# Two blocks of W2 converted inside the attention loop, on ScalarE and VectorE

## The chip, the cores and the metric

One of the cores of a Trainium2 chip runs the program; nothing is shared with other cores. The metric is the time of one execution on the device, in microseconds, taken as the median of several runs.

## The reference

Three layers follow one another on 4 batches of 576 tokens:

```python
# 1. attention, 8 heads of 64, causal window of 64
scores = q @ k.T / 8, masked to 0 <= i - j < 64
x = softmax(scores) @ v                               # [4, 576, 512]
# 2. gated unit with a spatial product
h = relu(x @ w_in); u, v = h[..., :512], h[..., 512:]
v = normalised(v) over its channels
x = (u * (w_spatial @ v + b)) @ w_out
# 3. mixer: tokens, then channels
u = x + w_tok2.T @ relu(w_tok1.T @ x)                 # per batch, over tokens
return u + relu(u @ w_c1) @ w_c2                      # w_c1 [512, 1536], w_c2 [1536, 512]
```

The weights arrive as 64-bit floats. The kernel multiplies in fp32 halves: every operand x is split into a high part hi (x rounded to fp32r) and a low part lo = x - hi, and a product takes three matmuls, hi·hi, hi·lo and lo·hi.

## The kernel before

**From 64-bit words to halves.** A weight tile comes by DMA as pairs of 32-bit words. `down` (L71, ScalarE) scales the high words as floats, `to_f32` (L60, VectorE) turns that into fp32 with one shift over the whole tile (L63) and two bit operations for each half of it (L68, L69), and `split` (L147) makes hi on ScalarE and lo on VectorE or GpSimd.

**Seven products for four.** The last product with w_c2, called W2 here, is done by quadrants of 256 columns with seven products in place of eight. So each of its six blocks j (rows 128j and 128(j+6) of W2, 128x1024 values) is not only converted: `load_c2` (L728) also forms four sums and differences of its quadrants (L738, GpSimd), splits all eight slots (hi on ScalarE, lo on GpSimd, L149), and stores hi and lo to a scratch tensor `scr` in DRAM (L742), from where `product` (L889) reads them (`w<-scr`). The raw words, the values and the halves live in 8 rotating buffers of 4 KB a partition, the pool `k4`. w_c1 has six such blocks too (`load_c1`, L699).

**Stages.** In the profiled execution:

- 0 to about 230 us: the attention with the first product of layer 2 woven in. This loop (L528) is written in the order in which each engine executes it (`manual_schedule`, L463). There are 18 tiles; turn n transposes the probabilities of tile n on TensorE (`att_turn`, L276), copies them (PT, L286, ScalarE), takes the eight exponentials of tile n+1 (`sexp`, L261, ScalarE), normalises tile n+1 (`snorm`, L267, VectorE: rs L272, L273, pb L274), multiplies tile n by v (`att_pv`, L289), and begins tile n+2 (`scores`, `smax`). So `snorm` waits on VectorE for the exponentials, and the next turn's transposes wait for `snorm`. Parts of w_spatial (ws, L101, L103) are converted at the ends of turns 2 to 5. Matmuls of `uv_v`, `uv_u` and `spatial` fill the rest of TensorE.
- about 230 to 364 us: the product with w_out (`wout`), the transposes back (`x2nat`), the token mixer (`tok1`, `tok2`), and beside them the conversion of w_t1, w_t2 and of nearly all blocks of w_c1 and W2. Here a scheduler sets the order on each engine; `load_c1` and `load_c2` are given a lower priority (`later`, L692). The list at L601 is the order in which the raw blocks are fetched.
- from about 364 us: the channel mixer, in three passes over 768 tokens.

The scheduler also puts work of the second stage into the engines' queues of the first where it fits: the first five pieces of w_out are fetched and converted (raw, val, wo_h, wo_l) during the attention.

`U` (L58) holds u of layer 2 for the four batches. Its columns 1152 to 2176 serve as landing space for raw w_in at the start (L460) and are written again by `uv_u` of the second pair of batches, from turn 12 on.

Of the kernel before, what the change touches and what calls it, by code (L numbers as in the profile page):

```python
# [20 lines left out]
P = 128  # L21
# [14 lines left out]
def tile_kernel(ctx, tc, qT, kT, kE, v, w_in, wsT, b_sp, w_out, w_t1, w_t2, w_c1, w_c2, outT):  # L36

    nc = tc.nc
# [32 lines left out]
    def down(x, high):  # L71
        nc.scalar.activation(out=x, in_=f(high), func=AF.Copy, scale=DOWN)
# [386 lines left out]
    def wv_part(k):  # L459
        return w_part(U[:, k, 1152:2176], w_in[128 * k:128 * k + 128, 512:].unsqueeze(1), wi_h[:, k:k + 1, 512:], wi_l[:, k:k + 1, 512:], 512)  # L460

    E = mybir.EngineType
    with tc.manual_schedule(engines={E.PE, E.SP, E.Activation, E.DVE, E.Pool}):  # L463
        wv = [wv_part(k) for k in range(4)]
# [2 lines left out]
        def go(*ws):  # L467
            for w in ws:
                next(w, 0)
# [54 lines left out]
        keep_busy(7, psa.tile([P, 512], F32, tag="xo", name="xo", bufs=1))  # L524
        uv_v(*its[0])
        conv, late = {1: (0,), 2: (1, 2), 3: (3,)}, ()
        ws_at = {2: 2, 3: 2, 4: 3, 5: 3}
        for n in range(1, len(its)):  # L528
            more, some = n + 2 < len(its), n + 1 < len(its)
            cv = [wu[i] for i in conv.get(n, ())]  # L530
            if n > 1:
                if n + 3 < len(its):
                    load_qk(n + 3)
                if more:
                    load_v(n + 2)
            PT = att_turn(n, busy={1: 2, 2: 8}.get(n, 0))
            go(*late)
            go(*late)
            go(*cv[:1])
            go(*cv[:1])  # L540
            if some:
                sexp(n + 1, 0)
                sexp(n + 1, 1)
                snorm(n + 1)
            go(*cv[:1])
            go(*cv[:1])
            tick()
            left = BUDGET - run_work(1)
            go(*cv[1:])
            att_pv(n, PT)  # L550
            go(*cv[1:])
            if more:
                scores(n + 2)
                smax(n + 2, 0)
                smax(n + 2, 1)
            if n > 1:
                tick()
            late = cv[1:]
            while work and left > 0:
                left -= run_work(1)  # L560
                tick()
            load_ws(ws_at.get(n, 0))
            enable(n)
        while turns:
            tick()
# [25 lines left out]
    def c1_source(j):  # L591
        return [w_c1[:, 128 * r:128 * r + 128].rearrange("(k p) c -> p k c", p=P) for r in (j, j + NJ)]

    def c2_source(j):
        return [w_c2[128 * r:128 * r + 128, :] for r in (j, j + NJ)]

    HW, TW, NJ = 384, 768, 6
    sources = [([w_t1[128 * k:128 * k + 256, :].rearrange("(k p) c -> p k c", p=P)], {}) for k in (0, 2)]
    sources += [([w_t1[512:, :]], dict(rows=64, dup=True))]
    sources += [([w_t2[128 * k:128 * k + 128, c0:c0 + 288]], {}) for k in range(2) for c0 in (0, 288)]  # L600
    sources += [(c1_source(j) if w == 1 else c2_source(j), {}) for w, j in  # L601
                ((2, 0), (1, 0), (2, 1), (2, 2), (1, 1), (1, 2), (2, 3), (1, 3), (2, 4), (1, 4), (1, 5), (2, 5))]
    issued = []

    def issue_next():
# [76 lines left out]
                mm3(ps[:, :288], [(ht[b][j][0][:, dc], ht[b][j][1][:, dc], t2_h[:, j, cs], t2_l[:, j, cs]) for j in range(2)])  # L682
                nc.vector.tensor_tensor(out=us, in0=ps[:, :288], in1=us, op=ALU.add)

    scr = tc.dram_tile([8, NJ // 2, P, 2, 2, 256], F32, name="scr")
    sums = tc.dram_tile([NJ, P, 4, 256], F32, name="sums")
    c1 = {}

# [39 lines left out]
    def load_c2(j):  # L728
# [5 lines left out]
        def blk(s, n=1):  # L734
            return Y[s // 4][:, s % 4:s % 4 + n, :]

        for o, a, b, op in ((4, 1, 3, ALU.add), (5, 4, 0, ALU.subtract), (6, 0, 1, ALU.subtract), (7, 2, 5, ALU.subtract)):
            nc.gpsimd.tensor_tensor(out=blk(o), in0=blk(a), in1=blk(b), op=op)  # L738
        for s, n in ((0, 1), (2, 2), (4, 2), (6, 2)):
            hl = kp.tile([P, 2, 2, 256], F32R, tag="k4", name="hl", bufs=8)[:, :n]  # L740
# [33 lines left out]

    wout(0)
    run_work(len(work))
    load_c2(0)
    wout(1)
    x2nat(0)
    load_c1(0)  # L780
    wout(2)
    tok1(0)
    load_c2(1)
    x2nat(1)
    wout(3)
    tok2(0)
    load_c2(2)
    load_c1(1)
    wout(4)
    x2nat(2)  # L790
# [261 lines left out]
```

## Time and profile before

| | |
|---|---|
| median of 3 runs | 638.13 us (638.07 to 638.38) |
| the profiled execution: time, span | 638.47 us, 636.7 us |
| TensorE (PE) busy | 610.3 us, 96% of the span |
| VectorE (DVE) busy | 459.5 us, 72% |
| ScalarE (ACT) busy | 334.1 us, 52% |
| GpSimd (POOL) busy | 153.4 us, 24% |
| granted TensorE clock | 1.00 (2.4 GHz) in all slices but the last |

Busy time counts an engine's own instructions. A row of the timeline gives the start, the duration, the engine, the line, the operation, the tiles as out<-in, and in brackets the idle time before it and what ended that. Matmuls overlap, so their durations are latencies, not costs. SyncE (SP) issues all DMAs in order; an issue row that lasts long is one that waited.

### The profile page before, as it was taken

What the parts mean: (1) busy time and instruction counts of PE and PEld (TensorE: products, weight loads), DVE (VectorE), ACT (ScalarE), POOL (GpSimd) and SP (SyncE); (2) the same over time, 40 slices, a digit from 0 to 9 for tenths busy, and PEclk for the clock granted to TensorE, in tenths of its full rate; (3) what the DMA queues carried; (4) which work ended last, traced back from release to release, by engine and by line L of the source; (5) the groups of instructions that cost most, each with busy time, mean ns of one, the idle gap of its engine ahead of it and who ended that gap; (6) DMA issues with size and microseconds to landing.
All of it is one profiled execution on the core that took longest, in us unless ns stands there. A gap on an engine that the chain in (4) does not pass through costs nothing.

```text
span 636.7 us, 12004 instructions
## 1 busy us (share of the span) xinstructions
PE 610.3 (96%) x4455; PEld 566.8 (89%) x4455; DVE 459.5 (72%) x977; ACT 334.1 (52%) x839; POOL 153.4 (24%) x166
## 2 busy tenths in 40 slices
PE   5889999999999999999899999999999999999997
PEld 2568798998889899888788899999999999999987
DVE  4896857556584688769978951278875998867982
ACT  4777853545674464666554442345543646344550
POOL 5610000100010010565475471041000440002510
PEclk9999999999999999999999999999999999999999
DMA  8853473222330135557756455057433675534772
GB/s 325 271 158 112 152 235 127 78 77 75 102 116 2 34 118 158 177 193 248 256 183 218 183 174 218 0 198 257 149 125 133 220 230 196 178 103 151 255 248 75
DMA packets 46106, 103.60 MB, mean 163 GB/s; under 512 B 4192, under 2 KB 16736, under 8 KB 46048
## 3 DMA queue, kind: packets, MB, share of 16 engines
q1 hardware_dynamic: 46048, 102.84, 48.3%
q8 instruction: 35, 0.57, 0.4%
q14 instruction: 23, 0.19, 0.1%
HBM read 83.95 MB, written 18.87 MB: 162 GB/s over the span
## 4 chain that ended last, share of the span: by engine, by line
PE 64%; DVE 14%; ACT 7%; DMA 5%; issue 4%; POOL 3%; SPq 1%; DVEq 0%; ACTq 0%; POOLq 0%
PE mm L161 27%; PE A L904 17%; PE mm L833 8%; PE A L833 6%; ACT pb L264 3%; DMA U<-in_w_in 3%; POOL k L738 2%; DVE k L68 2%; DVE k L69 2%; PE xo L297 2%; PE pt L285 2%; DMA scr<-hl 2%; DVE k L63 1%; PE A L161 1%; PE sc L241 1%
## 5 line engine op out<-in xcount | busy, mean ns | idle before, releaser
L904 PE MATMUL A<-oh,w 128*128 128x384 f32 x480 | 102.7, 334 | 0.0
L886 POOL TENSOR_TENSOR H<-H 128x384 f32<-128x384 f32 x36 | 45.0, 1264 | 184.9 <-DVE ol L899 171.0
L899 DVE TENSOR_TENSOR ol<-H,oh 128x384 fp32r<-128x384 f32 x120 | 77.2, 676 | 16.4 <-ACT oh L898 12.7
L904 PEld LDWEIGHTS A<-oh,w 128*128 128x128 f32 x480 | 85.0, 188 | 0.0
L898 ACT CAST oh<-H 128x384 fp32r<-128x384 f32 x120 | 60.0, 514 | 41.5 <-PE A L904 31.0
L904 PE MATMUL A<-ol,w 128*128 128x384 f32 x240 | 61.4, 336 | 2.2 <-DVE ol L899 2.2
L161 PE MATMUL mm<-ws,nh 128*128 128x288 f32 x320 | 62.0, 297 | 0.4 <-DVE tmp L394 0.4
L161 PEld LDWEIGHTS mm<-ws,nh 128*128 128x128 f32 x320 | 49.9, 188 | 1.0 <-DVE tmp L394 0.6
L363 POOL TENSOR_SCALAR rstd<-mv 128x1 f32<-128x1 f32 x18 | 4.9, 272 | 178.4 <-DVE mv L362 178.3
L904 PEld LDWEIGHTS A<-ol,w 128*128 128x128 f32 x240 | 43.1, 188 | 3.3 <-DVE ol L899 3.2
L886 DVE TENSOR_TENSOR H<-H 128x384 f32<-128x384 f32 x36 | 22.6, 628 | 21.8 <-ACT H L826 19.6
L161 PE MATMUL mm<-ws,nl 128*128 128x288 f32 x128 | 37.7, 295 | 0.0
L264 ACT ACTIVATE pb<-pb,nm 128x128 f32<-128x128 f32 x96 | 37.3, 400 | 0.4 <-DVE nm L255 0.4
L286 ACT COPY PT<-pt 128x512 f32<-128x512 f32 x36 | 19.4, 591 | 31.5 <-PE pt L285 31.5
L272 DVE TENSOR_SCALAR rs<-sm 128x8 f32<-128x8 f32 (+1 forms) x19 | 3.3, 172 | 42.9 <-ACT pb L264 42.9
L161 PE MATMUL mm<-xh,wi_h 128*128 128x384 f32 x96 | 32.7, 341 | 0.7 <-ACT vf L357 0.6
L161 PE MATMUL mm<-xh,wi_l 128*128 128x384 f32 x96 | 32.1, 334 | 0.0
L161 PE MATMUL mm<-xl,wi_h 128*128 128x384 f32 x96 | 32.1, 334 | 0.0
L161 PE MATMUL mm<-gh,wo_h 128*128 128x512 f32 (+1 forms) x80 | 29.4, 378 | 0.1
L161 PE MATMUL mm<-gh,wo_l 128*128 128x512 f32 (+1 forms) x80 | 29.4, 370 | 0.0
L161 PE MATMUL mm<-gl,wo_h 128*128 128x512 f32 (+1 forms) x80 | 29.4, 370 | 0.0
L149 POOL TENSOR_TENSOR hl<-k,hl 128x512 fp32r<-128x512 f32 (+1 forms) x24 | 28.6, 1208 | 0.0
(190 smaller groups left out, 1691.4 us busy)
## 6 DMA issues: line engine op xcount, KB each, us to landing
w<-scr SPq DMA_DIRECT2D x63, 512.0 KB, 4.4
k<-in_w_c SPq DMA_DIRECT2D x24, 512.0 KB, 5.3
scr<-hl SPq DMA_DIRECT2D x18, 512.0 KB, 6.1
kk<-in_kT SPq DMA_DIRECT2D x16, 384.0 KB, 4.7
k<-sums SPq DMA_DIRECT2D x12, 512.0 KB, 3.2
qq<-in_qT SPq DMA_DIRECT2D x18, 256.0 KB, 4.0
va<-in_v SPq DMA_DIRECT2D x18, 256.0 KB, 2.9
vb<-in_v SPq DMA_DIRECT2D x18, 256.0 KB, 3.9
```

The source lines that it names most:

```text
L68: nc.vector.scalar_tensor_tensor(out=y, in0=high, scalar=-0x80000000, in1=y, op0=ALU.bitwise_and, op1=ALU.bitwise_or)
L69: nc.vector.scalar_tensor_tensor(out=y, in0=low, scalar=29, in1=y, op0=ALU.logical_shift_right, op1=ALU.bitwise_or)
L149: eng.tensor_tensor(out=lo, in0=x, in1=f(hi), op=ALU.subtract)
L161: nc.tensor.matmul(o, a, c, start=(i == 0), stop=(i == n - 1))
L264: nc.scalar.activation(out=pb[:, h, :], in_=scs[g][:, h - 4 * g, :] if mk is None else pb[:, h, :], func=AF.Exp, scale=SCALE if mk is None ...
L285: nc.tensor.transpose(pt[:, h, :], pb[:, 4 * g + h, :], ident)
L286: nc.scalar.copy(out=PT[:, 4 * g:4 * g + 4, :], in_=pt)
L833: nc.tensor.matmul(o, a, m, start=first and i == 0, stop=i == len(todo) - 1, skip_group_check=True)
L886: eng.tensor_tensor(out=out, in0=a, in1=b, op=ALU.subtract)
L898: nc.scalar.copy(out=oh, in_=blk[j])
L899: nc.vector.tensor_tensor(out=ol, in0=blk[j], in1=f(oh), op=ALU.subtract)
L904: nc.tensor.matmul(acc[d], a, m, start=(first and j == 0 and i == 0), stop=(last and j == NJ - 1 and i == 2), skip_group_check=True)
```

## The change

Blocks 0 and 1 of W2 are no longer converted by `load_c2` in the second stage. A new generator `early_c2(j)` does each in seven steps, and the table `at` in the attention loop sets the turn and the point in the turn for each step: for block 0 the load at the end of turn 2, `down` in the middle of turn 3, `to_f32` ahead of the exponentials and `snorm` of turn 4, the four sums at that point of turn 5, the hi copies in the middle of turn 5, the lo differences at the exponentials of turn 6, and the stores to `scr` in the middle of turn 6; block 1 the same, four turns later. The sums and differences that were GpSimd's are VectorE's there. Raw words, values and halves all lie in the free columns of `U`, the halves in the space of the raw words and values that they replace; so block 1 can be loaded only when the first stores of block 0 have been read out. A block takes six stores in place of four, of rows of 1 KB in place of 2 KB. The other four blocks of W2 and the six of w_c1 keep their order, and the calls `load_c2(0)` and `load_c2(1)` are gone.

```diff
+    C2_SUMS = ((4, 1, 3, ALU.add), (5, 4, 0, ALU.subtract), (6, 0, 1, ALU.subtract), (7, 2, 5, ALU.subtract))
+    def early_c2(j):
...
+        for r, src in zip(raw, c2_source(j)):
+            nc.sync.dma_start(out=r, in_=src.bitcast(I32))
...
+        yield
+        for i, (low, high) in enumerate(parts):
+            down(span(2, 2 * i, 2), high)
+        yield
+        to_f32(span(2, 0, 4), parts)
+        yield
+        for o, a, b, op in C2_SUMS:
+            nc.vector.tensor_tensor(out=val[o], in0=val[a], in1=val[b], op=op)
+        yield
+        homes = ((2, 2, 0, 0, 2), (4, 2, 0, 2, 2), (6, 2, 1, 0, 2), (0, 1, 1, 2, 1))
+        for s, n, r, at, w in homes:
+            nc.scalar.copy(out=span(r, at, n).bitcast(F32R), in_=span(2 + s // 4, s % 4, n))
+        yield
+        for s, n, r, at, w in homes:
+            x = span(2 + s // 4, s % 4, n)
+            nc.vector.tensor_tensor(out=x.bitcast(F32R), in0=x, in1=span(r, at, n), op=ALU.subtract)
+        yield
+        for h, blocks in ((0, ((2, 4, 0, 0), (6, 2, 1, 0), (0, 1, 1, 2))), (1, ((4, 4, 3, 0), (2, 2, 2, 2), (0, 1, 2, 0)))):
+            for s, n, r, at in blocks:
+                nc.sync.dma_start(out=scr[s:s + n, j // 2, :, j % 2, h].rearrange("s p c -> p s c"), in_=span(r, at, n).rearrange("p (s c) -> p s c", c=256))
...
+        EARLY, FROM = 2, 2
+        side = [early_c2(j) for j in range(EARLY)]
+        at = {(FROM + 4 * j + t, point): side[j] for j in range(EARLY)
+              for t, point in ((0, "end"), (1, "mid"), (2, "exp"), (3, "exp"), (3, "mid"), (4, "exp"), (4, "mid"))}
...
             go(*cv[:1])
+            beside(n, "exp")
             if some:
                 sexp(n + 1, 0)
...
             if n > 1:
                 tick()
+            beside(n, "mid")
...
             load_ws(ws_at.get(n, 0))
+            beside(n, "end")
...
-                ((2, 0), (1, 0), (2, 1), (2, 2), (1, 1), (1, 2), (2, 3), (1, 3), (2, 4), (1, 4), (1, 5), (2, 5))]
+                ((1, 0), (2, 2), (1, 1), (1, 2), (2, 3), (1, 3), (2, 4), (1, 4), (1, 5), (2, 5))]
...
-    load_c2(0)
     wout(1)
     x2nat(0)
     load_c1(0)
     wout(2)
     tok1(0)
-    load_c2(1)
+    load_c2(2)
```

What this moves is shown at three places. First VectorE in turns 4, 5 and 6 (L272 to L274 are `snorm`; three pieces of the difference, between them nothing moves):

```order
 L103 TENSOR_TENSOR ws<-raw,ws 128x288 x2
+L63 TENSOR_SCALAR U<-U 128x1024
+L68 SCALAR_TENSOR_TENSOR U<-U 128x512
+L69 SCALAR_TENSOR_TENSOR U<-U 128x512
+L68 SCALAR_TENSOR_TENSOR U<-U 128x512
+L69 SCALAR_TENSOR_TENSOR U<-U 128x512
 L272 TENSOR_SCALAR rs<-sm 128x8
...
+L496 TENSOR_TENSOR U<-U 128x256 x4
 L272 TENSOR_SCALAR rs<-sm 128x8
...
+L504 TENSOR_TENSOR U<-U 128x512 x3
+L504 TENSOR_TENSOR U<-U 128x256
```

The five instructions of `to_f32`, the four sums and the four differences stand between the last work of the turn before and the `snorm` of tiles 5, 6 and 7.

Second SyncE's queue in turns 6 and 7, after the loads of v for tile 8:

```order
 L215 DMA va<-in_v 128x512
 L216 DMA vb<-in_v 128x512
+L508 DMA scr<-U 128x4x256
+L508 DMA scr<-U 128x2x256
+L508 DMA scr<-U 128x256
+L508 DMA scr<-U 128x4x256
+L508 DMA scr<-U 128x2x256
+L508 DMA scr<-U 128x256
+L486 DMA U<-in_w_c 128x1024 x2
 L200 DMA qq<-in_qT 128x512
 L203 DMA kk<-in_kT 128x768
```

The loads of q and k for tile 10, and behind them three loads of w_out (raw), now stand behind the six stores of block 0 and the two loads of block 1.

Third ScalarE in turn 7 (xh is the copy of tile 7's result, val the first step on w_out; a piece of the difference):

```order
 L264 ACTIVATE pb,sm<-pb,nm 128x128 x8
+L311 CAST xh<-xo 128x4x128
+L72 ACTIVATE U<-U 128x512 x2
 L72 ACTIVATE val<-raw 128x256 x2
-L311 CAST xh<-xo 128x4x128
```

`down` of block 1 (U<-U) now stands ahead of the first step on w_out. On VectorE that tile's next step (L63 val), which before stood within the `snorm` of tile 8, stands after it, ahead of xl of tile 7, the maxima of tile 9 and the `tmp` additions of `spatial` (L394). From the second stage on the scheduler's order differs on all engines; GpSimd's queue there has 16 instructions less and begins with block 0 of w_c1 (sums), no longer with block 0 of W2.

## Rows read from the trace of the kernel before

**Rows 1.** Windows by stage: start:end, length, busy us (instructions) by engine, PEclk, DMA.

```profile
80.00:230.00 150.00, 148.14 (x1426) 137.06 (x1425) 95.89 (x336) 78.06 (x267) 11.03 (x26) 1.00 0.30 91
230.00:412.00 182.00, 178.23 (x1035) 163.07 (x1034) 127.30 (x212) 91.92 (x171) 78.52 (x76) 1.00 0.53 185
```

**Rows 2.** Windows of the second stage (PE, PEld, DVE, ACT, POOL), then timeline rows.

```profile
300.00:312.00 12.00, 9.78 (x67) 8.62 (x66) 11.54 (x20) 5.28 (x10) 4.93 (x6) 1.00 0.80 295
312.00:364.00 52.00, 50.45 (x319) 45.81 (x318) 45.63 (x75) 27.03 (x47) 30.11 (x31) 1.00 0.57 201
...
302.19 1.05 ACT L148 CAST ws<-k 128x1024 fp32r<-128x1024 f32 x1 [2.68 <-DVE k L69]
304.33 0.40 PE L161 MATMUL mm<-t_h,hh 128*128 128x288 f32 x1 [1.42 <-ACT U L648]
309.24 0.40 PE L161 MATMUL mm<-t_h,hh 128*128 128x288 f32 x1 [0.57 <-DVE U L683]
```

**Rows 3.** Groups by form: shapes, count | busy us, mean ns | idle before, releasers.

```profile
L63 DVE TENSOR_SCALAR k<-k 128x1024 int32<-128x1024 int32 x12 | 12.9, 1075 | 13.5 <-ACT k L72 12.2 <-POOL hl L149 1.4
L68 DVE SCALAR_TENSOR_TENSOR k<-k,k 128x512 int32<-128x512 int32 x26 | 17.0, 684 | 0.2
L69 DVE SCALAR_TENSOR_TENSOR k<-k,k 128x512 int32<-128x512 int32 x26 | 18.4, 731 | 0.0
L335 DVE TENSOR_TENSOR nl<-vf,nh 128x512 fp32r<-128x512 f32 x16 | 11.0, 687 | 4.1 <-ACT nh L334 4.1
L103 DVE TENSOR_TENSOR wo_l<-val,wo_h 128x256 fp32r<-128x256 f32 x8 | 3.2, 414 | 0.0
L72 ACT ACTIVATE k<-k 128x512 f32<-128x512 f32 x26 | 16.7, 671 | 6.0 <-DMA k<-in_w_c 2.8 <-DMA k<-in_w_t 1.7 <-DMA scr<-hl 0.7
L148 ACT CAST hl<-k 128x512 fp32r<-128x512 f32 x18 | 11.2, 625 | 12.3 <-POOL k L738 9.9 <-DMA scr<-hl 1.9 <-DVE k L69 0.4
L149 POOL TENSOR_TENSOR hl<-k,hl 128x512 fp32r<-128x512 f32 x18 | 23.3, 1313 | 0.0
L738 POOL TENSOR_TENSOR k<-k 128x256 f32<-128x256 f32 x12 | 12.2, 1024 | 51.6 <-DVE k L69 51.6
```

**Rows 4.** Timeline of VectorE, then of TensorE, in turns 4 to 8.

```profile
58.33 0.83 DVE L103 TENSOR_TENSOR ws<-raw,ws 128x288 fp32r<-128x288 f32 x2 [1.48 <-ACT ws L101]
62.45 0.17 DVE L272 TENSOR_SCALAR rs<-sm 128x8 f32<-128x8 f32 x1 [3.29 <-ACT pb L264]
69.17 0.17 DVE L272 TENSOR_SCALAR rs<-sm 128x8 f32<-128x8 f32 x1 [0.78 <-ACT pb L264]
76.93 0.17 DVE L272 TENSOR_SCALAR rs<-sm 128x8 f32<-128x8 f32 x1 [0.84 <-ACT pb L264]
105.08 0.17 DVE L272 TENSOR_SCALAR rs<-sm 128x8 f32<-128x8 f32 x1 [3.57 <-ACT pb L264]
...
64.26 1.06 PE L285 MATMUL pt<-ident,pb 128*128 128x128 f32 x8 [1.23 <-DVE pb L274]
70.99 1.07 PE L285 MATMUL pt<-ident,pb 128*128 128x128 f32 x8 [0.80 <-ACT ws L101]
85.31 1.04 PE L285 MATMUL pt<-ident,pb 128*128 128x128 f32 x8
```

**Rows 5.** SyncE's timeline, then DMA issues: KB each, us to landing.

```profile
86.90 1.28 SPq L85 DMA_DIRECT2D raw<-in_w_out  x3
...
k<-in_w_c SPq DMA_DIRECT2D x24, 512.0 KB, 5.3
scr<-hl SPq DMA_DIRECT2D x18, 512.0 KB, 6.1
```

**Rows 6.** Timeline of VectorE and TensorE in turn 7.

```profile
95.48 0.69 DVE L312 TENSOR_TENSOR xl<-xo,xh 128x512 fp32r<-128x512 f32 x1
...
97.77 0.46 DVE L394 TENSOR_TENSOR tmp<-mm,bb 128x288 f32<-128x288 f32 x1
98.28 0.53 PE L161 MATMUL mm<-ws,nh 128*128 128x288 f32 x2 [0.36 <-DVE tmp L394]
```

More of the change, by code (lines that the diff above doesn't have):

```diff
@@ L460, in wv_part, with c2_source, span @@
         return w_part(U[:, k, 1152:2176], w_in[128 * k:128 * k + 128, 512:].unsqueeze(1), wi_h[:, k:k + 1, 512:], wi_l[:, k:k + 1, 512:], 512)
+    HW, TW, NJ = 384, 768, 6
+    scr = tc.dram_tile([8, NJ // 2, P, 2, 2, 256], F32, name="scr")
+    def c2_source(j):
+        return [w_c2[128 * r:128 * r + 128, :] for r in (j, j + NJ)]
+    C2_SUMS = ((4, 1, 3, ALU.add), (5, 4, 0, ALU.subtract), (6, 0, 1, ALU.subtract), (7, 2, 5, ALU.subtract))
+    def early_c2(j):
+        raw, hi, val = [], [], []
+        for k in range(4):
+            home = U[:, k, 1152:2176]
+            if k < 2:
+                raw.append(home.bitcast(I32))
+                hi += [home.bitcast(F32R)[:, 256 * i:256 * i + 256] for i in range(4)]
+            else:
+                val += [home[:, 256 * i:256 * i + 256] for i in range(4)]
+        def span(r, at, n):
+            return U[:, r, 1152 + 256 * at:1152 + 256 * at + 256 * n]
+        parts = []
+        for r, src in zip(raw, c2_source(j)):
+            nc.sync.dma_start(out=r, in_=src.bitcast(I32))
+            r3 = r.rearrange("p (n w) -> p n w", w=2)
+            parts.append((r3[:, :, 0], r3[:, :, 1]))
+        yield
[18 more added lines that the diff above has]
+                nc.sync.dma_start(out=scr[s:s + n, j // 2, :, j % 2, h].rearrange("s p c -> p s c"), in_=span(r, at, n).rearrange("p (s c) -> p s c", c=256))
     E = mybir.EngineType
@@ L526, in tile_kernel, with beside @@
         conv, late = {1: (0,), 2: (1, 2), 3: (3,)}, ()
+        EARLY, FROM = 2, 2
+        side = [early_c2(j) for j in range(EARLY)]
+        at = {(FROM + 4 * j + t, point): side[j] for j in range(EARLY)
+              for t, point in ((0, "end"), (1, "mid"), (2, "exp"), (3, "exp"), (3, "mid"), (4, "exp"), (4, "mid"))}
+        def beside(n, point):
+            if (n, point) in at:
+                next(at[n, point], 0)
         ws_at = {2: 2, 3: 2, 4: 3, 5: 3}
@@ L535, in tile_kernel @@
                     load_v(n + 2)
+            beside(n, "start")
             PT = att_turn(n, busy={1: 2, 2: 8}.get(n, 0))
@@ L592, in c1_source @@
         return [w_c1[:, 128 * r:128 * r + 128].rearrange("(k p) c -> p k c", p=P) for r in (j, j + NJ)]
-    def c2_source(j):
-        return [w_c2[128 * r:128 * r + 128, :] for r in (j, j + NJ)]
-    HW, TW, NJ = 384, 768, 6
     sources = [([w_t1[128 * k:128 * k + 256, :].rearrange("(k p) c -> p k c", p=P)], {}) for k in (0, 2)]
@@ L683, in tok2 @@
                 nc.vector.tensor_tensor(out=us, in0=ps[:, :288], in1=us, op=ALU.add)
-    scr = tc.dram_tile([8, NJ // 2, P, 2, 2, 256], F32, name="scr")
     sums = tc.dram_tile([NJ, P, 4, 256], F32, name="sums")
@@ L735, in blk @@
             return Y[s // 4][:, s % 4:s % 4 + n, :]
-        for o, a, b, op in ((4, 1, 3, ALU.add), (5, 4, 0, ALU.subtract), (6, 0, 1, ALU.subtract), (7, 2, 5, ALU.subtract)):
+        for o, a, b, op in C2_SUMS:
             nc.gpsimd.tensor_tensor(out=blk(o), in0=blk(a), in1=blk(b), op=op)
@@ L786, in tile_kernel @@
     tok2(0)
-    load_c2(2)
     load_c1(1)
```

## The prediction

> **What bounds the kernel now.** I read the stages first. Between 80 and 230 us TensorE is busy 148.14 of 150 us, between 230 and 412 us 178.23 of 182 [rows 1]: it is the bound nearly everywhere, and the granted clock is 1.00 in both stretches, 2.4 GHz. What a change of order can give back in the second stage is at most the 3.77 us in which TensorE is idle there. The second view shows where these lie: 2.22 us between 300 and 312 us, 1.55 between 312 and 364, none elsewhere that matters [rows 2]. A wait is a little longer than its idle time, since the last matmul's latency covers its start; I let that make the cap 5 us.
>
> The rows under the windows show how such a wait comes about. ScalarE sat 2.68 us before a w_c1 cast because VectorE had not finished that block's bit operations; behind the cast, in ScalarE's order, stood the eviction U L648 for which TensorE then waited 1.42 us [rows 2]. So conversion does not bound this stage by its sum (VectorE is busy 127.30 of 182 us, GpSimd 78.52 [rows 1]), but it makes the evictions late where VectorE is full: 11.54 of 12 us between 300 and 312 [rows 2].
>
> The third view is the timeline of VectorE in the attention. Ahead of each `snorm` it waits for the exponentials: 3.29, 0.78, 0.84 and 3.57 us in turns 4, 5, 6 and 8 [rows 4]. That is where the change puts its work. TensorE's side of the same rows says which of these waits have room behind them. In turns 5 and 6 the transposes start 1.81 and 1.82 us after rs and TensorE had been idle 1.23 and 0.80 us before them: it waits for `snorm`. In turn 7 they start 8.38 us after rs with no idle time: 6.6 us of room [rows 4].
>
> **What the change removes.** Two of twelve blocks leave the second stage: on GpSimd, for each, four sums and four differences, at most 4 x 1.02 + 3 x 1.31 + 1.0 = 9.0 us (the difference of half size put at a sum's 1.0), so 17 to 18 us in all; on VectorE 1.08 + 2 x 0.68 + 2 x 0.73 = 3.9 us each; on ScalarE two passes `down` of 0.67 and hi copies of about 3 x 0.63 + 0.4, 3.6 us each [rows 3]. None of it is on TensorE, so none of it counts by itself. What counts is the idle 3.77 us. Bounds: nothing returns, if the scheduler's new order puts an eviction behind a conversion elsewhere; all 5 us return, if VectorE's 7.8 us less and the earlier start of the rest keep every eviction on time. Ten of twelve blocks are still there and still share queues with the evictions, so not all waits go. I take the waits of 300 to 312 us, **-2.2 us**, and leave those after 312.
>
> **What it adds in the attention, block 0.** `to_f32` in turn 4: 3.9 us, each step waiting for the one before, starts when the two ws differences end at 59.16 and takes the place of an idle 3.29 us: `snorm` is late by 0.6 us, and TensorE, which waits for it, by the same [rows 3, 4]. The four sums in turn 5: 0.41 each, less a little for overlap (two ws differences of 0.45 took 0.83 together [rows 4]), 1.5 us in an idle 0.78: late by 0.7 us, again with TensorE waiting [rows 3, 4]. The shift of 0.6 us does not change that idle time, since the exponentials of tile 6 follow the late transposes. Together **+1.3 us**. Bounds: 0.8, if the steps overlap by 0.1 each, and 2.0, if the ScalarE copies of turn 5, 2.3 us ahead of the ws casts and the PT copies, also delay att_pv. The four differences in turn 6: 3 x 0.69 + 0.41 = 2.5 us in an idle 0.84, 1.6 us late, against 6.6 us of room [rows 3, 4]: nothing. If that cover were gone they would cost 1.6. `down` in turn 3 costs 1.3 us on ScalarE, off TensorE's path.
>
> **Block 1.** Its `to_f32` takes 3.9 us in an idle 3.57 [rows 3, 4], 0.3 us late where TensorE is full (148.14 of 150 us [rows 1]): nothing. Its sums and differences come in turns 9 and 10, in the same full stretch: nothing.
>
> **The queue in turns 6 and 7.** The six stores and two loads have a cost of another kind. SyncE issues in order, so the load of block 1 waits there until the first stores of block 0 have landed, and the loads of w_out, issued at 86.90 before [rows 5], wait behind it. ScalarE's `down` of block 1 waits for that load with the val pass queued behind; VectorE's L63 on val waits for ScalarE with the maxima of tile 9 and a `tmp` addition behind; and for that addition, at 97.77, TensorE already waits 0.36 us [rows 6]. In numbers: the differences of turn 6 end near 79.5, with the shift 81; a first store lands after 6.1 us, 87, the reload after another 5.3, 92.5, the second a little later, 94; two `down` of 0.67 [rows 3, 5] bring 95.3, the val pass about 96. L63 on val must run some 2.9 us before `tmp`: xl and the maxima take 2.3 (95.48 to 97.77 [rows 6]), itself and one addition in between some 0.6; so by 94.9, with the shift of 1.3 by 96.2. So it is just in time; I take **+0.2 us**. Bounds: 0, and 3, if the stores (2 MB in rows of 1 KB, a shape no store of the trace has) and the loads take half as long again.
>
> A rule of the Trainium skill speaks against the change here. "DMA: Bandwidth & Descriptors", section "Anatomy of one DMA", says that DMA engines do not wait on semaphores and that a wait happens on the issuing sequencer before dispatch; it says too that the fixed cost is mostly the write receipt, the longest towards HBM. By that rule the loads behind the waiting reload are held up although the DMA engines may be free, which is the slower rival below.
>
> A second page asks for a larger gain: "GPSIMD Engine Reference", section "Specifications", says that GpSimd shares its SBUF interfaces with VectorE and contends with two-input VectorE instructions. By that rule VectorE would also get faster as 17 us of GpSimd work go. No run here shows it yet: the two-input L335 of 128x512, which runs in the attention where GpSimd is busy 11.03 of 150 us, takes 687 ns, L68 of the same size beside GpSimd 684 [rows 1, 3], so I give it nothing.
>
> **The sum.** -2.2 + 1.3 + 0.2 = -0.7 us, against the profiled execution's 638.47: 637.8. That execution lies 0.34 us over the median of 638.13, so I predict 637.4. About 0.2%, 1.3 us, is what a measurement of this kernel can tell from no change: the forecast lies within it.
>
> **The rivals.**
>
> - *The relief is worth more* (faster). Without two blocks the rest starts some 15 us earlier, VectorE is less full where the evictions come, and nearly all the idle time goes: -5 + 1.3 + 0.2, or -3.5 at best, some -2.5 with a wait left: 634.6 to 635.7. For it: one eviction behind one conversion made the largest wait [rows 2]. Against: short tiles of the token mixer leave little time for each eviction whatever is converted.
> - *The queue is late* (slower). The reload lands after about 94.8, each further microsecond goes through val, the maxima and `tmp` to TensorE, and at 3 us late the sum is -2.2 + 1.3 + 3 = +2.1: 640.2. It decides from the point where val is ready later than 96.2. For it: four steps wait for one another with no slack, and TensorE is idle before `tmp` already [rows 6]. Against: the median landing times just do.
> - *Nothing returns in the second stage*. The scheduler makes another order, with other evictions behind other conversions: 0 + 1.3 + 0.2 = +1.5: 639.6.
> - *The attention does not pay either.* If the instructions in U overlap more than those in k, or the exponentials are later than thought, 0.8 in place of 1.3: 636.9, within the forecast's own range.
>
> **How the numbers follow.** The forecast, with the last case, has 0.38; the larger relief 0.37; the late queue 0.14; no return 0.11. The first gives "within 0.2%", the second "faster", the others "slower". The range goes from 634.7, nearly the best case, to 640.1, nearly the late queue's 3 us, and leaves out the further ends; the forecast's own range is 636.9 to 639.4.
>
> **What would show it.** In turns 4 and 5 VectorE no longer waits before rs, and TensorE's idle times of 1.23 and 0.80 before the transposes grow to about 1.85 and 1.5. GpSimd's busy time falls by some 17 us. The reload of block 1 lands before 95, and TensorE's wait for `tmp` near 98 stays under 0.8. Between 230 and 412 us, shifted by 1.5, TensorE's idle time falls from 3.77 to about 1.5. If it stays above 3, or that wait passes 2 us, the forecast is wrong on the slow side; if it falls under 0.5, on the fast side.

## The result, and the profile after

The kernel after takes **643.81 us** (median of 6 runs, 641.42 to 644.61), the kernel before, on the same chip, 638.40 (638.07 to 639.25). The ratio is 1.0076, 95% interval 1.0055 to 1.0097: slower by 3.5 to 6.2 us, where 637.4 was forecast, and above the range's upper end of 640.1. Two of the six executions took 641.42 and 641.77; the one with a trace took 644.16 us, 5.69 more than the profiled one of before.

| profiled execution | before | after |
|---|---|---|
| time, span | 638.47, 636.7 us | 644.16, 642.3 us |
| TensorE busy | 610.3 us | 612.4 us |
| VectorE busy | 459.5 us | 465.4 us |
| GpSimd busy | 153.4 us | 136.5 us |
| mean granted clock | 1.000 | 0.995 |

GpSimd's 17 us went as forecast. The windows by stage of after answer to [rows 1] and [rows 2] (columns as there). The second stage begins 6.4 us later in after, as the ledger below shows, so the two windows that answer to [rows 2] are moved by as much:

```profile
80.00:230.00 150.00, 144.53 (x1396) 133.47 (x1395) 99.38 (x336) 77.67 (x265) 8.96 (x22) 0.99 0.37 122
230.00:412.00 182.00, 178.31 (x1040) 163.69 (x1039) 124.80 (x217) 87.17 (x165) 65.36 (x65) 1.00 0.45 154
...
306.40:318.40 12.00, 11.51 (x83) 10.90 (x82) 10.24 (x19) 6.49 (x14) 5.98 (x6) 1.00 0.92 307
318.40:370.40 52.00, 49.03 (x306) 44.58 (x305) 41.06 (x66) 23.40 (x41) 23.48 (x24) 1.00 0.57 198
```

The first stage lost, and the second gained nothing. TensorE is idle 5.47 us between 80 and 230 us, 1.86 in before. In the second stage it is idle 3.69 us, 3.77 in before: of the 2.22 us between 300 and 312 us 0.49 is left, and the 1.55 after 312 grew to 2.97.

Where the first stage lost is one place. These are the timeline rows of after on SyncE, ScalarE, VectorE and TensorE in turns 6 to 8:

```profile
82.44 5.23 SPq L508 DMA_DIRECT2D scr<-U  x6
88.78 1.38 SPq L486 DMA_DIRECT2D U<-in_w_c  x2
91.15 0.91 SPq L85 DMA_DIRECT2D raw<-in_w_out  x2
...
93.50 0.67 ACT L72 ACTIVATE U<-U 128x512 f32<-128x512 f32 x1 [0.47 <-DMA U<-in_w_c]
95.16 0.66 ACT L72 ACTIVATE U<-U 128x512 f32<-128x512 f32 x1 [0.99 <-DMA U<-in_w_c]
98.77 0.43 ACT L72 ACTIVATE val<-raw 128x256 f32<-128x256 f32 x1 [2.95 <-DMA raw<-in_w_out]
...
99.23 0.29 DVE L63 TENSOR_SCALAR val<-val 128x256 int32<-128x256 int32 x1 [3.95 <-ACT val L72]
...
103.14 0.40 PE L161 MATMUL mm<-ws,nh 128*128 128x288 f32 x1 [3.97 <-DVE tmp L394]
```

and the transfer as the chain of waits has it (start, duration):

```profile
91.15 7.60 DMA raw<-in_w_out
```

Read from the top: six stores, which take SyncE 5.23 us to issue (5.22 in dma_alone, where none of their issues is listed as waiting, so a long issue row need not be one that waited), the reload of block 1, for which SyncE waits 1.7 us until stores have landed, and only then w_out's raw words, issued at 91.15 and landed at 98.75. ScalarE has long done its `down` of block 1 and waits 2.95 us for them, VectorE waits 3.95 us for ScalarE, and behind L63 stand the maxima and the `tmp` for which TensorE waits 3.97 us; it was 0.36 in before [rows 6]. What follows is a second loss, in the windows of after:

```profile
90.00:100.00 10.00, 9.18 (x116) 8.54 (x115) 3.56 (x9) 5.15 (x18) 0.00 (x0) 1.00 1.04 388
104.00:106.00 2.00, 2.00 (x10) 2.00 (x9) 1.97 (x6) 0.00 (x0) 0.00 (x0) 0.50 0.51 136
106.00:108.00 2.00, 2.00 (x13) 1.98 (x13) 1.72 (x5) 0.82 (x2) 0.00 (x0) 0.65 0.39 126
```

In the first row the DMA engines are full for 10 us, a share of 1.04 at 388 GB/s. In the other two the granted clock, 1.00 until then, stands at 0.50 and 0.65 in the mean: 1.2 GHz behind the wait, and ten matmuls in 2 us where engines_alone, a kernel of the experiments without this wait, has 18 in the same window.

A **ledger** puts a size on each. An execution's start varies (tile 4's transposes begin between 56.3 and 59.7 us in the profiled runs), so I count from tile 4's first transpose to tile 17's, and from there to the end of the span. The rows of after are

```profile
57.83 0.49 PE L285 MATMUL pt<-ident,pb 128*128 128x128 f32 x3
...
64.96 0.41 PE L285 MATMUL pt<-ident,pb 128*128 128x128 f32 x2 [1.24 <-DVE pb L274]
72.28 0.41 PE L285 MATMUL pt<-ident,pb 128*128 128x128 f32 x2 [1.39 <-DVE pb L274]
...
215.18 0.49 PE L285 MATMUL pt<-ident,pb 128*128 128x128 f32 x3
```

and those of before

```profile
57.15 0.49 PE L285 MATMUL pt<-ident,pb 128*128 128x128 f32 x3
...
208.78 0.49 PE L285 MATMUL pt<-ident,pb 128*128 128x128 f32 x3
```

| kernel | tile 4 to tile 17 | against before | tile 17 to the end |
|---|---|---|---|
| before | 151.63 | | 427.9 |
| after | 157.35 | +5.72 | 427.1 |
| dma_alone | 157.15 | +5.52 | 427.7 |
| no_hold | 157.34 | +5.71 | 427.5 |
| engines_alone | 152.17 | +0.54 | 427.8 |
| hold12 | 152.29 | +0.66 | 427.1 |
| later5 | 154.71 | +3.08 | 428.2 |
| wait2 | 157.02 | +5.39 | 427.1 |
| wait4 | 158.43 | +6.80 | 427.6 |
| filled | 155.42 | +3.79 | 428.5 |
| stores_after | 152.15 | +0.52 | 428.3 |
| best | 151.77 | +0.14 | 427.8 |
| best_p3 | 151.82 | +0.19 | 427.0 |
| best_p0 | 151.77 | +0.14 | 426.0 |

After's 5.72 us are the wait (3.97 - 0.36 = 3.61), the four sums of block 0 (idle time before tile 6's transposes 1.39 in place of 0.80, so 0.59) and a rest of 1.52, which the experiments give to the clock. The two windows of low clock give about the same: 2 us at 0.50 and 2 us at 0.65 are 1.0 + 0.7 = 1.7 us lost. With a start 0.68 us later and an end 0.8 shorter that makes 5.6 of the 5.69.

### The profile page after: what moved, and what is told of

It is laid out like the page before. It is cut to its first block, busy times and chain, and to the rows that moved or that the text cites. A ratio compares the mean times of both kernels' runs of the same rounds, so it can differ in the third digit from the quotient of the medians.

```text
span 642.3 us, 12011 instructions
## 1 busy us (share of the span) xinstructions
PE 612.4 (95%) x4455; PEld 569.0 (89%) x4455; DVE 465.4 (72%) x993; ACT 333.7 (52%) x839; POOL 136.5 (21%) x150
## 4 chain that ended last, share of the span: by engine, by line
PE 71%; DVE 10%; ACT 6%; DMA 6%; issue 3%; SPq 1%; POOL 1%; DVEq 0%; ACTq 0%; POOLq 0%
PE mm L161 31%; PE A L958 18%; PE mm L887 8%; PE A L887 6%; ACT pb L264 2%; DMA kk<-in_kT 2%; PE A L161 2%; PE pt L285 2%; PE xo L297 2%; PE sc L241 1%; DMA raw<-in_w_out 1%; DVE k L68 1%; DVE pb L274 1%; DVE k L69 1%; DMA scr<-U 1%
## 5 line engine op out<-in xcount | busy, mean ns | idle before, releaser
L940 DVE TENSOR_TENSOR H<-H 128x384 f32<-128x384 f32 x36 | 21.0, 583 | 25.1 <-ACT H L880 22.9
L880 ACT ACTIVATE H<-mm 128x384 f32<-128x384 f32 x24 | 11.7, 492 | 34.0 <-PE mm L161 33.9
L990 DVE TENSOR_TENSOR U<-A,U 128x384 f32<-128x384 f32 x42 | 21.9, 550 | 10.0 <-PE A L958 5.5
```

The source lines that it names most:

```text
L880: nc.scalar.activation(out=t, in_=ps, func=AF.Relu)
L940: eng.tensor_tensor(out=out, in0=a, in1=b, op=ALU.subtract)
L990: nc.vector.tensor_tensor(out=at, in0=src, in1=at, op=ALU.add)
```

## The experiments

Two theories stood at the start: **the late queue** (DMAs in turns 6 and 7 make w_out's raw words late) and **the engines' work** (the ScalarE and VectorE steps themselves hold up TensorE). Every ratio is against the kernel before on the same chip.

**One half of the change at a time.** dma_alone takes from `early_c2` its loads and stores only:

```diff
+        for r, src in zip(raw, c2_source(j)):
+            nc.sync.dma_start(out=r, in_=src.bitcast(I32))
...
+                nc.sync.dma_start(out=scr2[s:s + n, j // 2, :, j % 2, h].rearrange("s p c -> p s c"), in_=span(r, at, n).bitcast(I32).rearrange("p (s c) -> p s c", c=256))
```

> The kernel before, with the two early blocks' DMAs alone at their places (two loads and six stores for each, of the words as loaded, into a scratch tensor that nothing reads); no conversion is added in the attention, and the second stage still converts all twelve blocks. Theory A, the queue is late: stores and reload ahead of w_out's raw words in SyncE's order make val late; TensorE waits 2.5 us or more for tmp near 98 us, the granted clock falls behind that wait, and the time is 3 to 5.5 us over before, 641.4 to 644. Theory B, the added ScalarE and VectorE steps make the loss: no wait for tmp over 1 us, and the time within 1 us of before's 638.4.

engines_alone takes the rest, and no DMA:

```diff
+            down(span(2, 2 * i, 2), high)
...
+        to_f32(span(2, 0, 4), parts)
...
+            nc.vector.tensor_tensor(out=val[o], in0=val[a], in1=val[b], op=op)
...
+            nc.scalar.copy(out=span(r, at, n).bitcast(F32R), in_=span(2 + s // 4, s % 4, n))
...
+            nc.vector.tensor_tensor(out=x.bitcast(F32R), in0=x, in1=span(r, at, n), op=ALU.subtract)
```

> The kernel before, with the early blocks' ScalarE and VectorE steps alone, worked on whatever lies in those words of U, and none of their DMAs; the second stage still converts all twelve blocks. Theory A, the queue is late: SyncE's order is that of before, so no wait over 1 us for tmp near 98 us and no clock below 0.9 near 105; what is left is the sums' 0.6 us before the transposes of turn 5, so 638.4 to 639.7. Theory B, the engine steps make the loss: TensorE waits 3 us or more between 90 and 110 us, and the time is 641.5 to 644.

dma_alone took 643.06 us, ratio 1.0080 (1.0064 to 1.0095), engines_alone 638.64, ratio 1.0013 (1.0002 to 1.0024). The DMAs alone make the whole loss, with the wait and the clock. TensorE's wait in dma_alone, and then the window behind it:

```profile
100.87 0.85 PE L161 MATMUL mm<-ws,nh 128*128 128x288 f32 x2 [3.16 <-DVE tmp L394]
```

```profile
102.00:104.00 2.00, 2.00 (x10) 2.00 (x10) 1.75 (x5) 0.00 (x0) 0.00 (x0) 0.50 0.57 169
```

The same two views of engines_alone:

```profile
101.36 0.53 PE L161 MATMUL mm<-ws,nh 128*128 128x288 f32 x2 [0.34 <-DVE tmp L394]
```

```profile
104.00:106.00 2.00, 2.00 (x18) 2.00 (x17) 1.90 (x5) 2.00 (x8) 0.00 (x0) 1.00 0.00 0
```

What engines_alone loses, 0.54 us in the ledger, is the sums' share. The rival theory falls.

**The waiting step taken away.** hold12 leaves the DMAs of after and keeps w_out's second group from being fetched before turn 12:

```diff
+            if n == 12:
+                for _ in range(3):
+                    nc.gpsimd.memset(stage.tile([P, 2 * WN], F32, tag="raw", name="hold")[:, :1], 0.0)
```

> The kernel after, with w_out's second group of raw loads and its val steps held back until turn 12 (three one-column clears of the raw buffers on GpSimd). Theory A, the loss is one wait, of tmp queued behind val, and the clock behind it: with no val step near 98 us the wait of 3.97 us and the clock of 0.50 at 104 to 106 us both go, tile 8's first transposes come at 101 to 102 us, and the time is 638 to 639.5. Theory B, block 1's ScalarE and VectorE steps between 95 and 110 us are what TensorE waits for, through the exponentials or snorm: the wait only changes its name, and the time stays over 641.

It took 639.31 us, ratio 1.0021 (1.0011 to 1.0030). The wait near 98 us and the low clock are gone, and tile 8's transposes come at 100.74. The val step now costs 0.7 us elsewhere: its two ScalarE passes, at 167.56 and 168.96, stand ahead of the copies of tile 13 and the exponentials of tile 14, and tile 14's transposes wait 1.47 us, 0.78 in before.

**Order or bandwidth.** The raw words could be late because SyncE issues them late, behind a reload that waits for stores to land, or because the DMA engines are full. later5 puts block 1 one turn later, so that its reload stands behind them:

```diff
-        at = {(FROM + 4 * j + t, point): side[j] for j in range(EARLY)
+        at = {(FROM + 5 * j + t, point): side[j] for j in range(EARLY)
```

> The kernel after, with all steps of block 1 one turn later: its two loads now stand behind w_out's raw loads in SyncE's order, while block 0's six stores still stand ahead of them. Theory A1, w_out's loads were held in SyncE's order behind the reload's wait for the stores: they are issued near 87 us and land by 95 us, the wait for tmp is under 1 us, and the time is 638 to 640. Theory A2, the DMA engines' bandwidth made them late (the stores' 1 KB rows fill it): they land at 97 us or later whatever the order, the wait stays over 2 us, and the time is over 641.

It took 642.47 us, ratio 1.0065 (1.0049 to 1.0082), which neither theory had quite: issued at 87.47, as A1 has it, the words still took 5.73 us (the chain of waits), and 93.2 lies between the two. Its profiled execution is the fastest of its four (641.12). VectorE's L63, which in this kernel stands within `snorm` as in before, waits 2.40 us, and TensorE twice:

```profile
95.53 0.53 PE L161 MATMUL mm<-ws,nh 128*128 128x288 f32 x2 [1.59 <-DVE tmp L394]
100.50 0.53 PE L161 MATMUL mm<-ws,nh 128*128 128x288 f32 x2 [0.98 <-DVE tmp L394]
```

Behind these two the granted clock stayed at 1.00. no_hold takes away SyncE's wait ahead of the reload. It is dma_alone with block 1 in other columns of U, which no store of block 0 reads:

```diff
-        for r, src in zip(raw, c2_source(j)):
+        base = 2 * (j % 2)
+        for r, src in zip([U[:, base + k, 1152:2176].bitcast(I32) for k in range(2)], c2_source(j)):
```

> As dma_alone (the kernel before with the early blocks' DMAs alone, to a scratch tensor that nothing reads), but block 1's words are loaded over words of U that no store of block 0 reads, so that its loads do not wait for those stores to land; the bytes and the order of the DMAs are the same. Theory A, the wait of SyncE before the reload is what made w_out's loads late: they are issued 1.4 us earlier than in dma_alone and land by 92 us, TensorE's wait for tmp is under 1.5 us and the time 638.5 to 640.5. Theory B, the DMA engines are full with stores and reload whatever SyncE waits for: they still land at 95 us or later, the wait is 2 to 3.5 us, and the time 641 to 643.5.

It took 643.84 us, ratio 1.0097 (1.0077 to 1.0118). SyncE no longer waits ahead of the reload, and the first raw load, which ScalarE's first val pass waits for, is issued at 88.40, 1.63 us earlier than in dma_alone (90.03; 0.24 of it because the stores began that much earlier here). It lands no earlier, at 96.81 in place of 96.5. A wait of 2.2 us for the stores has not gone: it now stands ahead of the second and the third raw load (89.91 and 91.46, 90.56 and 91.12 in dma_alone), but the first is not touched by it. The chain of waits and then TensorE's row in no_hold:

```profile
88.40 8.41 DMA raw<-in_w_out
```

```profile
101.20 0.85 PE L161 MATMUL mm<-ws,nh 128*128 128x288 f32 x2 [3.82 <-DVE tmp L394]
```

What SyncE no longer waits ahead of that load is added to its transfer: theory B, with wait and time a little over its bounds of 3.5 and 643.5. In before the five such loads of this stretch took 3.1 us in the median, from the view of DMA issues:

```profile
raw<-in_w_out SPq DMA_DIRECT2D x5, 256.0 KB, 3.1
```

stores_after draws the consequence: the stores of block 0 and all of block 1 a turn later, so that the three raw loads stand ahead of both.

```diff
-        at = {(FROM + 4 * j + t, point): side[j] for j in range(EARLY)
-              for t, point in ((0, "end"), (1, "mid"), (2, "exp"), (3, "exp"), (3, "mid"), (4, "exp"), (4, "mid"))}
+        at = {(FROM + 5 * j + t, point): side[j] for j in range(EARLY)
+              for t, point in ((0, "end"), (1, "mid"), (2, "exp"), (3, "exp"), (3, "mid"), (4, "exp"), (5, "mid"))}
```

> The kernel after, with block 0's stores one turn later and all steps of block 1 one turn later, so that w_out's first three raw loads stand ahead of all six stores in SyncE's order. Theory A, stores and loads that share the DMA engines with w_out's raw loads make the loss: those land 2.9 to 3.5 us after their issue, the wait for tmp is under 0.8 us, the clock stays 1.00, and the time is the sums' 0.6 us less what the second stage gives back, 0.7: 637.5 to 638.8. Theory B, the conversion itself delays TensorE in turns 7 to 12 whatever the order of the DMAs: over 640.

It took 639.30 us, ratio 1.0012 (1.0001 to 1.0023), 0.5 us over theory A's upper end. The attention is as expected. The raw loads of this stretch and TensorE's row for `tmp` in stores_after:

```profile
raw<-in_w_out SPq DMA_DIRECT2D x5, 256.0 KB, 3.3
99.19 0.40 PE L161 MATMUL mm<-ws,nh 128*128 128x288 f32 x1 [0.34 <-DVE tmp L394]
```

The ledger has +0.52 us, all of it the sums'. So the same transfers, put behind the raw loads, cost nothing there. Whether the bytes of the stores or their rows of 1 KB fill the DMA engines was not varied.

What did not come is the second stage's 0.7 us, which I had read from single spans of after and hold12 (427.1). In the ledger's last column the six kernels that still convert all twelve blocks there range from 427.1 to 427.9, and those that convert ten, best_p0 aside, from 427.0 to 428.5. The three highest, stores_after, later5 and filled (428.2 to 428.5), are those in which the granted clock falls once in the second stage, as the next part shows; the other four have 427.0 to 427.8, no clear difference from twelve blocks. In stores_after the clock stands at 0.66 in the mean from 328 to 333 us, a loss of 5 x 0.34 = 1.7 us, so without that fall its profiled 639.80 would lie inside theory A's range.

**The price of the wait and of the clock.** wait2 and wait4 change no transfer; they add five and ten additions on VectorE ahead of one `tmp` of before (the diff is wait2's):

```diff
+            for _ in range(5 if (b, d, c0) == (0, 1, 0) else 0):
+                nc.vector.tensor_tensor(out=tmp, in0=bb[:, cs], in1=bb[:, cs], op=ALU.add)
```

> The kernel before, with five needless additions on VectorE (tmp of the bias with itself, overwritten by the addition that follows) ahead of the tmp that comes at 97.77 us in before; no DMA is changed. It prices a short wait by itself. Theory A, a wait costs its own length while the granted clock holds, and the clock falls behind a long one: TensorE waits some 2.2 us there (0.4 plus 5 x 0.37), the clock stays 1.00, and the time is 1.5 to 2.3 us over before. Theory B, the clock falls behind any wait of this kind: it shows 0.5 in the 4 us that follow, and the time is 3.5 us over before or more.

> As wait2, with ten such additions. Theory A: TensorE waits 3.9 to 4.3 us there, the granted clock falls to 0.5 for some 3 us behind the wait as in the kernel after, and the time is 3.6 us for the wait and 1.5 to 2 for the clock over before, 5.1 to 5.8 in all. Theory B, the low clock in the kernel after had to do with its stores and not with the wait: the clock stays 1.00, and the time is 3.4 to 3.9 us over before.

wait2 took 642.29 us, ratio 1.0069 (1.0049 to 1.0088), wait4 645.42, ratio 1.0112 (1.0097 to 1.0127). The additions, which all write the same tile, took 0.49 us each, not 0.37, so the waits were longer than meant. TensorE's row and then the window behind it, in wait2:

```profile
102.46 0.85 PE L161 MATMUL mm<-ws,nh 128*128 128x288 f32 x2 [3.08 <-DVE tmp L396]
```

```profile
104.00:106.00 2.00, 2.00 (x11) 1.98 (x10) 0.58 (x2) 0.00 (x0) 0.00 (x0) 0.50 0.00 0
```

and in wait4 the wait:

```profile
104.28 0.85 PE L161 MATMUL mm<-ws,nh 128*128 128x288 f32 x2 [5.55 <-DVE tmp L396]
```

The clock falls with no transfer added. Of the ledger's +5.39 in wait2 the wait is 3.08 - 0.36 = 2.72 and the rest, 2.67, the clock's; of the +6.80 in wait4 the wait is 5.19, the rest 1.61. wait4's median is 7.4 us over before, more than its 5.1 to 5.8, since the wait was longer. wait2 was to be a short wait without the fall and was not, so its theory A is untested at its own length.

Which waits bring the clock down, these runs do not settle. In the attention it fell behind 3.08 us and all longer waits (3.16, 3.82, 3.97, 5.55) and held behind 1.59 and 0.98 in later5. But in the second stage one and the same wait, for the eviction hl, goes both ways. TensorE's row and the window behind it, in stores_after and then in hold12:

```profile
328.07 0.40 PE L161 MATMUL mm<-t_h,hl 128*128 128x288 f32 x1 [1.51 <-DVE hl L729]
329.00:332.00 3.00, 3.00 (x15) 3.00 (x14) 2.28 (x3) 2.21 (x3) 2.70 (x3) 0.50 0.64 199
...
328.54 0.40 PE L161 MATMUL mm<-t_h,hl 128*128 128x288 f32 x1 [1.52 <-DVE hl L732]
329.00:332.00 3.00, 3.00 (x25) 3.00 (x24) 2.48 (x4) 2.19 (x3) 2.24 (x3) 1.00 0.58 207
```

It fell behind that wait in stores_after, later5 and filled, and held in after, hold12 and best_p3, with 1.51 or 1.52 us in all six. The length of a single wait does not decide it alone.

filled goes the other way. It is after, with TensorE given work in that place: the group of 14 matmuls ahead of the wait is computed three times over.

```diff
+            for _ in range(3 if (b, d, c0) == (0, 2, 0) else 1):
+                mm3(ps[:, :288], [(vn[b, s][0][:, dc], vn[b, s][1][:, dc], ws_h[:, s, cs], ws_l[:, s, cs]) for s in range(4)],
+                    [(vtl, ws_h[:, 4, cs]), (vtl, ws_l[:, 4, cs])])
```

> The kernel after, with one matmul group of the mixer (the one ahead of the wait for tmp, 14 matmuls, 1.87 us) computed three times over in place, so that TensorE works through the time in which it waited 3.97 us; the late queue itself stays. Theory A, the clock fell because TensorE stood idle, and cost 1.5 us or more beside the wait: the wait shrinks to some 0.3 us, the granted clock stays 1.00 from 98 to 110 us, and the time is 1.5 to 2.5 us under the kernel after, 640.2 to 642.3, though the same work waits for the same transfers. Theory B, the clock's part is small: the time stays within 0.7 us of the kernel after.

It took 642.14 us, ratio 1.0063 (1.0050 to 1.0076), 1.7 us under after's median (0.8 by the two ratios, whose intervals overlap, so the time alone does not settle it) though TensorE does 3.74 us more work. The windows of filled:

```profile
98.00:104.00 6.00, 6.00 (x46) 5.86 (x45) 5.42 (x27) 0.88 (x2) 0.00 (x0) 1.00 0.41 160
104.00:108.00 4.00, 4.00 (x34) 4.00 (x33) 3.86 (x9) 2.92 (x13) 0.00 (x0) 1.00 0.38 126
```

TensorE is never idle, the clock stays 1.00 in this stretch, and the ledger falls by 1.93, from +5.72 to +3.79. Of that 0.23 is the difference between the wait of 3.97 and the work of 3.74, so the clock's part is 1.7 us in this pair, near the 1.52 that remained of after's ledger.

**The sums out of the way.** best is stores_after with the four sums behind `snorm`, where no transposes wait for them, and the steps that follow later too:

```diff
-              for t, point in ((0, "end"), (1, "mid"), (2, "exp"), (3, "exp"), (3, "mid"), (4, "exp"), (5, "mid"))}
+              for t, point in ((0, "end"), (1, "mid"), (2, "exp"), (3, "mid"), (4, "mid"), (5, "exp"), (5, "mid"))}
```

> As stores_after, and the four sums of each block half a turn later, behind snorm, with the two ScalarE passes and the four differences half a turn to a turn later too, so that no TensorE wait of turn 5 lies behind the sums. If the ledger is right (sums 0.57 us, second stage 0.7 back), TensorE's idle time before the transposes of turn 6 is 0.8 us as in before and the time is 637.0 to 637.8, at or just under before. If the sums' 0.57 us was not theirs, it stays as in stores_after.

It took 638.60 us, ratio 1.0009 (0.9998 to 1.0020), 0.8 us over the upper end of what was expected. The idle time before tile 6's transposes is 0.75 us, so the 0.59 was the sums'; the second stage again gives nothing, and the time is that of before.

**Why the second stage gives nothing.** In after, TensorE's largest wait there and VectorE's rows ahead of it are these:

```profile
333.62 0.40 PE L161 MATMUL mm<-t_h,hl 128*128 128x288 f32 x1 [1.52 <-DVE hl L729]
```

```profile
330.11 0.68 DVE L63 TENSOR_SCALAR k<-k 128x1024 int32<-128x1024 int32 x1
330.82 0.69 DVE L343 TENSOR_TENSOR nh<-A,nh 64x512 fp32r<-64x512 f32 x1
331.55 1.29 DVE L68 SCALAR_TENSOR_TENSOR k<-k,k 128x512 int32<-128x512 int32 x2
332.87 0.69 DVE L729 SCALAR_TENSOR_TENSOR hl<-A,hh 128x512 fp32r<-128x512 f32 x1
```

It is a wait of the kind of [rows 2]: an eviction (hl of the token mixer) behind a conversion (k). In before TensorE waits 0.72 us for the same hl; here it is 1.52, while the wait of 1.42 for U is gone. best_p0 and best_p3 move the place where the stage's first W2 block is called for, earlier and later. best_p0 also fetches that block's raw words first, as before did with block 0; best_p3 leaves the fetches alone. This is best_p0's change against best:

```diff
-                ((1, 0), (2, 2), (1, 1), (1, 2), (2, 3), (1, 3), (2, 4), (1, 4), (1, 5), (2, 5))]
+                ((2, 2), (1, 0), (1, 1), (1, 2), (2, 3), (1, 3), (2, 4), (1, 4), (1, 5), (2, 5))]
...
     run_work(len(work))
+    load_c2(2)
     wout(1)
...
     tok1(0)
-    load_c2(2)
```

> The kernel best, with the second stage's first w_c2 block converted earlier, where the kernel before converted block 0, so that no conversion is called for between the first channel mixer step and its successor. Theory A, the second stage gives nothing back because the wait of before only moved to other evictions (of hl, hh, U) that stand behind conversions: with this one moved, TensorE's idle time between 230 and 412 us falls from 3.7 to 2.5 or less and the time to 636.5 to 637.8. Theory B, some eviction stands behind some conversion wherever they are called for: idle time 3.2 to 4.5 us, and 638 to 639.3 as best.

> As best_p0, with that block converted later than in best, where the kernel before converted its third w_c2 block. The theories and their numbers are the same: 636.5 to 637.8 with 2.5 us or less of TensorE idle time between 230 and 412 us by A, 638 to 639.3 by B.

best_p3 took 639.25 us, ratio 1.0014 (1.0001 to 1.0027), with 3.59 us idle: theory B for that place. best_p0 took **636.17 us, ratio 0.9971 (0.9960 to 0.9981)**, faster than both kernels, with 2.03 us idle: theory A. The stage's window in best, the same in best_p0, and best_p0's VectorE:

```profile
230.00:412.00 182.00, 177.72 (x1035) 162.84 (x1034) 117.95 (x202) 84.42 (x160) 63.11 (x61) 1.00 0.45 153
```

```profile
230.00:412.00 182.00, 179.97 (x1048) 165.08 (x1047) 118.17 (x205) 87.33 (x163) 62.78 (x61) 1.00 0.44 153
```

```profile
326.29 0.69 DVE L63 TENSOR_SCALAR k<-k 128x1024 int32<-128x1024 int32 x1
327.01 0.69 DVE L729 SCALAR_TENSOR_TENSOR hl<-A,hh 128x512 fp32r<-128x512 f32 x1
327.62 1.28 DVE L68 SCALAR_TENSOR_TENSOR k<-k,k 128x512 int32<-128x512 int32 x2
```

hl now runs ahead of L68, and TensorE's wait for it is 0.67 us, 1.17 in best. The rest of the 2.25 us less of idle time is spread over the waits for hh (0.86 to 0.31) and nl (0.56 and 0.71, both gone). best_p0 keeps before's first call and first fetch and drops the two calls behind it; so two blocks less are worth some 1.6 us there (427.6, the mean of the six kernels with all twelve, against 426.0 in best_p0's one trace), where the calls that go are the right ones. Whether the call or the fetch decides, no run separates, and that evictions stood behind just these conversions is shown for hl only.

## Why the prediction was wrong

**What bounds the kernel** held: TensorE, with waits in single places, and the place of the loss was among those named.

**The failed step is the queue in turns 6 and 7**, taken at +0.2 us with bounds of 0 and 3. It measured 3.6 us of wait and some 1.5 of clock. Two of the signs named beforehand said so: the wait for `tmp` passed 2 us (3.97), and the idle time of the second stage stayed above 3 (3.69). The chain of landings failed in its last link. I had the stores at 81, the reload at 92.5 and 94, and w_out's words no later than the reload. The stores were issued at 82.44 and the reload's two halves landed by 93.50 and 95.16, about a microsecond late. But the raw words, the loads behind them, had no transfer time of their own in the sum; they took 7.60 us, where 3.1 is what such loads took in before. Half as long again, the bound set for stores and loads, would have allowed them 4.6. The mistake was to price transfers by their durations in the trace of before: 1.75 MB of stores (seven of the eight slots of a block are stored, so not 2 MB) and 1 MB of reload were put ahead of them, and the DMA engines ran full.

The Trainium skill's rule that I weighed there ("DMA: Bandwidth & Descriptors", section "Anatomy of one DMA", written for DMAs that GpSimd issues: a wait happens on the issuing sequencer) agrees with the trace, where SyncE waits 1.7 us for the stores before it has issued the reload. But no_hold shows that this wait cost nothing: the first raw load, issued earlier without it, landed no earlier. I had looked at the queue, and the DMA engines were what was full.

**The clock** had no term at all. The Trainium skill has the rule, in "TensorE: Matmul & The Clock Gate", section "Part 1: The HAM clock gate": the array's clock depends on how busy it has lately been, and it runs at 1.2 GHz when it was idle. The trace agrees: the granted clock was 0.50 behind the wait of 3.97 us. A rival whose price is a wait of several microseconds on TensorE should carry it.

**The second stage's -2.2 us** came as 0. The reading of [rows 2] was right about the cause, an eviction behind a conversion, and it was the rival "nothing returns" that came true: the waits of 300 to 312 us mostly went (2.22 to 0.49 us), others grew behind them (1.55 to 2.97). best_p0 shows that most of the size was to be had (about -1.6), with another order of calls and fetches.

**The attention's +1.3 us** measured 0.6. The four sums cost 0.59 where 0.7 was forecast. (The row of before names ws on ScalarE, not `snorm`, as what ended the wait before tile 6's transposes; `snorm` ended 0.1 us ahead of it.) `to_f32` cost nothing where 0.6 was forecast: idle time before tile 5's transposes is 1.24 us, 1.23 in before. VectorE's rows of after show why:

```profile
59.76 0.69 DVE L63 TENSOR_SCALAR U<-U 128x1024 int32<-128x1024 int32 x1
...
63.15 0.17 DVE L272 TENSOR_SCALAR rs<-sm 128x8 f32<-128x8 f32 x1
```

Five instructions took 3.4 us, not 3.9, and rs came as the exponentials ended. L63 took 0.69 us, not the 1.08 of [rows 3], which is a mean over two kinds, see the last section. The differences of turn 6 and all of block 1 cost TensorE nothing, as forecast.

**The rival "the queue is late"** was the right mechanism, place and point of decision (val ready later than 96.2; its second pass on ScalarE ended at 99.84), with a chance of 0.14. Its price of 640.2 assumed the -2.2 us and no clock; with what was measured for the attention, the wait and the clock, and nothing from the second stage, the same sum gives 638.13 + 0.6 + 3.6 + 1.5 = 643.8. The rival of a larger relief (its 635.7 should read 635.6, 638.13 - 2.5) did not come.

## What to carry to other kernels

When work is moved earlier, list the transfers that it puts ahead of others in the same microseconds and add up their bytes: here the loads behind landed only when what stood ahead had been moved, and issuing the first of them 1.4 us earlier did not help. A wait of TensorE of some microseconds can cost more than its length, because the clock may fall behind it; look at the granted clock behind every wait before you put a difference down to anything else. And relieving an engine in a stage that is bound by single waits gave time back here with only one of three places tried for the first W2 call, so look which work stands ahead of the late instruction before you choose what leaves.

## What the runs showed of the hardware

- Behind five of TensorE's waits, of 3.08 to 5.55 us, the granted clock stood at 0.50 for 3 to 6 us after matmuls resumed, and cost 1.5 to 2.7 us beside the wait. Behind a wait of 1.51 or 1.52 us it fell to 0.50 for some 3 us in three traces and held at 1.00 in three. In the profiled pair of after and filled, two useless matmul groups in place of the wait cost less than the wait and the clock behind it (+3.79 against +5.72 us in the ledger).
- With the DMA share at 1.04 and 388 GB/s over 10 us (after), a 256 KB load took 7.60 us, and 8.41 where it was issued earlier (no_hold); such loads took 3.1 in before and 3.3 in stores_after, in the median.
- L63 over 128x1024 took 0.68 to 0.69 us whenever no GpSimd instruction ran beside it (9 of the 24 in the traces of before and after), and 0.75 to 1.69 beside one (15). Two rows of before, and GpSimd's last rows ahead of the second:

```profile
326.73 1.69 DVE L63 TENSOR_SCALAR k<-k 128x1024 int32<-128x1024 int32 x1 [1.30 <-ACT k L72]
336.32 0.68 DVE L63 TENSOR_SCALAR k<-k 128x1024 int32<-128x1024 int32 x1
```

```profile
324.06 3.81 POOL L149 TENSOR_TENSOR hl<-k,hl 128x512 fp32r<-128x512 f32 x3
...
333.09 2.55 POOL L716 TENSOR_TENSOR k<-k,k 128x256 f32<-128x256 f32 x2
```

  The first L63 begins within L149's 3.81 us; the second begins 0.68 us after GpSimd's last instruction ended. The Trainium skill, "GPSIMD Engine Reference", section "Specifications", says that GpSimd shares its SBUF interfaces with VectorE and contends with VectorE instructions that have two SBUF inputs or run in a mode of two ports. The trace agrees that this instruction is slower beside GpSimd; it has one input, and whether it runs in such a mode no row shows. So the mean in [rows 3] was too high a price for a place where GpSimd is still.
